# Third pair's rotation in an attention-and-experts kernel: VectorE sums GpSimd's products, and TensorE turns the pair one block later

## The chip, the cores and the metric

The kernel runs on one core of one Trainium2 chip. The core's engines have queues of their own and run beside each other: TensorE (PE in the rows, PEld for its weight loads), VectorE (DVE), ScalarE (ACT), GpSimd (POOL) and SyncE (SP, which here only issues transfers). Each queue is worked through in order, and an instruction whose input is late holds up all that stands behind it on its engine. The metric is the device time of one execution in microseconds (us), lower is better.

## The reference

Attention with rotary positions over 8 batches, 8 heads, 576 positions and 64 values per head, and a mixture-of-experts layer on its 4608 rows:

```python
def rotate(x):
    x1, x2 = (x[..., :half], x[..., half:])
    return np.concatenate([x1 * cos - x2 * sin, x1 * sin + x2 * cos], axis=-1)
q_rot, k_rot = (rotate(q), rotate(k))
scores = scale * np.matmul(q_rot, k_rot.transpose(0, 1, 3, 2))
scores = scores - np.max(scores, axis=-1, keepdims=True)
attn = np.exp(scores)
attn = attn / (np.sum(attn, axis=-1, keepdims=True) + 1e-09)
out = np.matmul(attn, v)
...
h_dense = np.maximum(x @ w1_dense, 0.0)
y_dense = h_dense @ w2_dense
expert_idx = np.argmax(logits, axis=1)
...
    h = np.maximum(x[mask] @ w1[e], 0.0)
    y_moe[mask] = gate_w[mask, None] * (h @ w2[e])
return y_dense + y_moe
```

## The kernel before, in words

The 64 heads are worked through as 32 pairs, `i` = 0 to 31. For each pair the steps are these.

- **Load**: `stage_load` brings q and k of two pairs at a time into a tile `qk` (SP's queue).
- **Rotation** (`stage_rope`): three products of `qk` with the tables `cosx` and `sinx` (lines 253, 254 and 255), in bf16, and their sum into the pair's tile `nat` (line 256). Pairs 0 and 1 are rotated by VectorE, with the products in a tile named `rab`; all others by GpSimd, with the products in tiles `ra` and `rb`, of which there is one each. There are three `nat` tiles, taken in turn.
- **Turn**: pairs 0, 1 and 2 are transposed by TensorE (`turn_first`, line 277, four pieces n = 0 to 3) and copied out by ScalarE (line 278) into `q1` and `k2`. From pair 3 on the turn is a transposing DMA (`stage_transpose`, line 263), and a second DMA moves the keys to their own tile (`stage_keys`, line 281, in the rows `k<-q`). Both are issued by SP.
- **First scores** (`s1_block`, lines 288 to 291): nine blocks `t` of query-major scores; VectorE takes the row maximum of each block (line 305, and 311 for the small piece of block 4). `s1_rest` does the last 64 keys (line 319), `join_max` the join (line 326). The blocks of the pairs up to 6 use four PSUM banks in turn: those tagged `s1` for even blocks, those tagged `ff` for odd ones and for the small piece of block 4.
- **Shift** (`shift_rows`): the maxima are turned by TensorE (line 333), fitted by ScalarE and VectorE (lines 337 and 338, tile `mT`) and written by an SP transfer (line 339) into two rows of `q1`, so that the second product subtracts them.
- **Second scores** (`s2_strip`, lines 346 to 349) with ScalarE's exponential (line 361), product with v (`av_part`, line 380) and scaling on VectorE (lines 391 and 392).

The order is written out by hand. `attention()` begins with two loops that do the first scores of pairs 0 and 1 and put the turns of pairs 1 and 2 between their blocks. After that the main loop runs over `i` and `t`: it does the first scores of pair `i + 2`, the second scores of pair `i` and the product with v of pair `i - 1`, and from the fifth turn or so fills TensorE with work of the dense and expert layers. The rotation of pair `i + 5` is put into GpSimd's queue at block 2 of turn `i`; those of pairs 3 and 4 stand ahead of the main loop. In this text **turn i** is one round of the main loop, and it is cut at the end of VectorE's join of maxima (line 326), which happens once per round.

Of the kernel before, what the change touches and what calls it, by code (L numbers as in the profile page):

```python
# [24 lines left out]
def kernel(  # L25
# [12 lines left out]
    nc = tc.nc  # L38
# [107 lines left out]
    state = {}  # L146
# [58 lines left out]
    def load(dst, src, b, hh):  # L205
        nc.sync.dma_start(dst.rearrange("p u (a j) d -> p (u a) (j d)", a=2)[:, :, 0:4 * D],
                          src[b, 4 * hh:4 * hh + 4, 0:MAIN, :].rearrange("h (p j) d -> p h (j d)", j=4))
        for a in range(2):
            nc.sync.dma_start(dst[64 * a:64 * a + 64, :, 4, :],
                              src[b, 4 * hh + a:4 * hh + a + 3:2, MAIN:S, :].rearrange("h p d -> p h d"))  # L210

    def stage_load(g, part):
        b, hh = divmod(g, 2)
        if part == 0:
            state["qk", g] = ap.tile([P, 2, 2, 10, D], f32, tag="qk", bufs=3, name="qk")
        load(state["qk", g][:, part], (q, k)[part], b, hh)
# [23 lines left out]
    def stage_rope(i):  # L240
        eng = nc.vector if i < 2 else nc.gpsimd
        g, u = divmod(i, 2)
        nat = nats[i % NAT].rearrange("p c w d -> p w c d")
        x = state["qk", g][:, :, u, 0:9]
        if i < 2:
            r = ap.tile([P, 5, DG], f32, tag="xn", bufs=2, name="rab").rearrange("p j d -> p (j d)")
            a, s = (r[:, n * 9 * D:(n + 1) * 9 * D].bitcast(bf16).rearrange("p (w c d) -> p w c d", w=2, d=D)
                    for n in range(2))
        else:
            a, s = (ap.tile([P, 2, 9, D], bf16, tag=n, bufs=1, name=n) for n in ("ra", "rb"))  # L250
        cx_ = cosx[:, None].broadcast_to([P, 2, 9, D])
        sx = sinx[:, None].broadcast_to([P, 2, 9, D])
        eng.tensor_tensor(a, x, cx_, AL.mult)  # L253
        eng.tensor_tensor(s[:, :, :, 0:half], x[:, :, :, half:D], sx[:, :, :, 0:half], AL.mult)  # L254
        eng.tensor_tensor(s[:, :, :, half:D], x[:, :, :, 0:half], sx[:, :, :, half:D], AL.mult)  # L255
        eng.tensor_tensor(nat, a, s, AL.add)  # L256

    A0, B0 = 0, S
# [8 lines left out]
    def turn_first(i, n):  # L267

        nat = nats[i % NAT]
        if n == 0:  # L270
            state["q1", i] = ap.tile([P, QC], bf16, tag="q1", bufs=NK, name="q1")
        c0, c1 = ((0, 4), (4, 9))[n // 2]
        w, dst = ((2, state["q1", i]), (1, k2s[i % NK]))[n % 2]
        r = w * D
        ps = pp.tile([P, 8, P], bf16, tag="ff" if w == 1 and i < 2 else "s2", bufs=2, name="nps")
        for c in range(c0, c1):
            nc.tensor.transpose(ps[0:r, c - c0], nat[:, c, 2 - w:2, :].rearrange("p w d -> p (w d)"), ident_b)
        nc.scalar.copy(dst[0:r, c0 * P:c1 * P], ps[0:r, 0:c1 - c0].rearrange("p c d -> p (c d)"))
# [15 lines left out]
    def s1_block(i, t):  # L294
        if t == 0:
            state["negm", i] = ap.tile([P, 10, 2], f32, tag="negm", bufs=3, name="negm")
        def bank(n):
            return "ff" if i < 7 and n % 2 else "s1"

        tag = bank(t)  # L300
        ps = pp.tile([P, MAIN], f32, tag=tag, bufs=2, name="s1")
        s1_mm(i, t, ps, 0)
        spend(512 if t != 4 else 800)
        banks[tag].append(took("dve", 0.6, product(0.22 if t != 4 else 0.32, tag)))
        nc.vector.tensor_reduce(state["negm", i][:, t, 0:1], ps, axis=AX.X, op=AL.max, negate=True)  # L305
        if t == 4:
            tag = bank(1)
            ps = pp.tile([P, MAIN], f32, tag=tag, bufs=2, name="s1")
            s1_mm(i, t, ps[:, 0:TAIL], 1)
            banks[tag].append(took("dve", 0.14, product(0.03, tag)))  # L310
            nc.vector.tensor_reduce(state["negm", i][:, t, 1:2], ps[:, 0:TAIL], axis=AX.X, op=AL.max, negate=True)
# [657 lines left out]
    MORE = 2900  # L969

    def attention():
        for i in range(2):
            for t in range(9):
                s1_block(i, t)
                if i == 0 and 2 <= t < 6:
                    turn_first(1, t - 2)
                if i == 1 and 3 <= t < 7:
                    turn_first(2, t - 3)
                if (i, t) == (1, 1):
                    shift_rows(0)  # L980
                    stage_load(3, 1)
                    dense = [load_w(n, w1d, moe_w1_dense) for n in range(DT)]
                    for u in range(HP):
                        cast_v(0, u)
            s1_rest(i)
            join_max(i)
        stage_rope(3)
        stage_rope(4)
        stage_transpose(3)
        AV = {2: (0, 2), 3: (2, 5), 6: (5, 7), 7: (7, 10)}  # L990
# [16 lines left out]
        for b in range(1, B):  # L1007
            for u in range(HP):
                i = 4 * (b - 1) + u - (b == 2)
                if b == 1:  # L1010
                    if u > 1:
                        when(u - 1, 6, 0, lambda u=u: stage_v(1, u, u + 1))
                    i, t = ((1, 8), (2, 4), (3, 3), (3, 8))[u]
                else:
                    when(i, 6, 0, lambda b=b, u=u: stage_v(b, u, u + 1))
                    i, t = i + 2, 3
# [6 lines left out]
        for b in range(B - 1):  # L1023
            s = 4 * b
# [60 lines left out]
        b, i = B - 1, NP - 1  # L1085
# [42 lines left out]
    with tc.manual_schedule():  # L1128
        load_pair(0, 0, nc.sync)
        load_pair(0, 1, nc.sync)  # L1130
        load_pair(1, 0, nc.sync)
        load_pair(1, 1, nc.sync)
        stage_load(1, 0)
        stage_load(1, 1)
        psi, sc = tables()
        nc.gpsimd.tensor_copy(ident_b, ident_f)
        nc.gpsimd.tensor_copy(ident_h, ident_f)
        for x in (cx, tops, gall):
            nc.gpsimd.memset(x, 0.0)
        gate_constants()  # L1140
        pad_tails()
        load_gate()
        pad_keys(0)
        tables_done(psi, sc)
        pad_keys(1)
        pad_keys(2)
        stage_v(0)
        stage_load(2, 0)
        stage_load(2, 1)
        stage_rope(0)  # L1150
        for n in range(4):
            turn_first(0, n)
        for x in range(3, NK):
            pad_keys(x)
        stage_rope(1)
        hold = const_p.tile([1, 1], bf16, name="hold")
        nc.gpsimd.tensor_copy(hold, nats[1][0:1, 0, 0, 0:1])
        stage_rope(2)
        stage_load(3, 0)
        setup_cm.__exit__(None, None, None)  # L1160
        attention()

        L = state["L"]
        n_rest = nc.values_load(L[-1][0:1, 0:1], min_val=0, max_val=B * (E - 1))
        with tc.If(n_rest > 0):
            for n in range(1, NREST + 1):
                with tc.If(n_rest >= n):
                    pick_rest(L, n)
                    picked()
                    load_rest()  # L1170
                    gate_rest(nc.vector, DT)
                    queue.extend(rest_items())
                    fill(1 << 30)
# [30 lines left out]
```

## Time and profile before

| what | us |
|---|---|
| median of three runs (lowest, highest) | 421.92 (421.78, 422.32) |
| the profiled execution, its own time | 423.38 |
| span of the profiled execution, first to last instruction | 421.80 |
| TensorE busy | 384.4 (91%) |
| VectorE busy | 332.5 (79%) |
| ScalarE busy | 307.4 (73%) |
| GpSimd busy | 295.7 (70%) |

The profile is of one execution. The shares are means over stages with different limits, so a change in one stage is read from that stage's rows. In a row of the timeline, the first number is the start after the span's first instruction, the second the length, and the bracket at the end is the idle time of the engine before it and what ended that.

### The profile page before, as it was taken

The page shows a single profiled execution, that of the slowest core. Times are in us where ns is not written, and L with a number is a line of the kernel's source. Part 1 is how long each engine was busy: PE and PEld are TensorE (multiplying, and loading weights), DVE is VectorE, ACT ScalarE, POOL GpSimd, SP SyncE. Part 2 cuts the span into 40 slices and gives each one's busy share as a digit, 9 for nine tenths or more (in the row PEclk, how much of TensorE's full clock was granted, in tenths as well). Part 3 has the DMA queues.
Part 4 walks back from the last instruction along what each step waited for, and adds up shares of the span by engine and source line. Part 5 has one row for each costly group of instructions (what it writes and reads, how often), then busy time and mean ns, then how long its engine had stood idle before and what let it go on. Part 6 is the DMA issues. An engine that isn't in the chain of part 4 may idle for free. (4 is left out here: it accounts for less than half of the span.)

```text
span 421.8 us, 11454 instructions
## 1 busy us (share of the span) xinstructions
PE 384.4 (91%) x4483; PEld 231.7 (55%) x4488; DVE 332.5 (79%) x794; ACT 307.4 (73%) x623; POOL 295.7 (70%) x212
## 2 busy tenths in 40 slices
PE   0777888998999999999999999999999899998992
PEld 0433455664665557565665556655656566566551
DVE  7987999999799888998799887988899777623740
ACT  7767787787868887788877886788777787774311
POOL 3499999999996999579984999299947000470220
PEclk9988999999999999999999999999999999999998
DMA  4995677699777996599587876698438910697842
GB/s 123 269 268 131 130 140 181 150 205 187 181 166 148 217 177 195 168 223 181 130 222 164 219 175 164 162 212 177 102 79 184 131 58 16 177 203 117 189 129 87
DMA packets 99329, 68.91 MB, mean 163 GB/s; under 512 B 55742, under 2 KB 91838, under 8 KB 99264
## 3 DMA queue, kind: packets, MB, share of 16 engines
q1 hardware_dynamic: 88928, 57.71, 54.8%
q0 software_dynamic: 10192, 10.23, 16.6%
q8 instruction: 37, 0.61, 0.6%
q14 instruction: 28, 0.23, 0.2%
q10 hardware_dynamic: 144, 0.13, 0.1%
HBM read 50.22 MB, written 14.42 MB: 153 GB/s over the span
## 5 line engine op out<-in xcount | busy, mean ns | idle before, releaser
L305 DVE TENSOR_REDUCE negm<-s 128x1 f32<-128x512 f32 x288 | 192.4, 684 | 38.1 <-PE s L291 36.5
L361 ACT ACTIVATE pm<-s 128x512 f16<-128x512 f32 x288 | 170.6, 600 | 58.5 <-PE s L349 50.9
L349 PE MATMUL s<-q,k 128*128 128x512 bf16 (+1 forms) x507 | 105.1, 286 | 5.7 <-ACT pm L361 3.8
L291 PE MATMUL s<-k,q 126*128 126x512 bf16 x256 | 98.2, 388 | 4.9 <-DVE negm L305 2.2
L253 POOL TENSOR_TENSOR ra<-qk,cosx 128x1152 bf16<-128x1152 f32 x30 | 78.8, 2627 | 2.9 <-DMA qk<-in_k_dram 1.4
L380 PEld LDWEIGHTS <-pm 128*128 128x128 f16 x1600 | 65.3, 98 | 24.9 <-issue 3.0
L256 POOL TENSOR_TENSOR nat<-ra,rb 128x1152 bf16<-128x1152 bf16 x30 | 70.9, 2363 | 2.4
L380 PE MATMUL av<-v,pm 128*128 128x65 f16 x1600 | 71.3, 194 | 0.5 <-DVE xn L392 0.3
L514 POOL DMA_DIRECT2D w1e<-in_moe_w_dram x8 | 6.4, 800 | 81.9 <-DVE early L811 38.0
L349 PEld LDWEIGHTS <-k 128*128 128x128 bf16 x512 | 36.9, 98 | 37.1 <-issue 10.4
L291 PEld LDWEIGHTS <-q 126*128 126x128 bf16 x512 | 35.4, 98 | 29.8 <-issue 9.7
L254 POOL TENSOR_TENSOR rb<-qk,sinx 128x576 bf16<-128x576 f32 x30 | 42.1, 1403 | 0.0
L255 POOL TENSOR_TENSOR rb<-qk,sinx 128x576 bf16<-128x576 f32 x30 | 42.0, 1400 | 0.0
L608 PE MATMUL yps<-w2e,he 128*128 128x512 f16 x124 | 36.7, 379 | 0.0
L608 PE MATMUL yps<-w2d,hd 128*128 128x512 f16 x124 | 36.5, 378 | 0.0
L557 PE MATMUL hps<-xh,w1d 128*128 128x512 f16 x128 | 35.9, 379 | 0.0
L557 PE MATMUL hps<-xg,w1e 128*128 128x512 f16 x128 | 35.6, 379 | 0.0
L591 POOL TENSOR_TENSOR xg<-xh,gB 128x2304 f16<-128x2304 f16 x7 | 32.1, 4584 | 1.9 <-ACT gB L531 1.6
L392 DVE TENSOR_TENSOR xn<-av,rz 128x320 f32<-128x320 f32 x64 | 31.5, 492 | 2.2
L370 ACT ACTIVATE pm<-s 128x64 f16<-128x64 f32 x64 | 26.2, 410 | 0.0
L612 ACT COPY y<-yps 128x512 f32<-128x512 f32 x31 | 18.2, 587 | 8.3 <-PE yps L608 7.8
L414 DVE TENSOR_TENSOR xl<-xps,xh 128x512 f16<-128x512 f32 x32 | 21.8, 682 | 3.0 <-ACT xh L410 3.0
(211 smaller groups left out, 559.3 us busy)
## 6 DMA issues: line engine op xcount, KB each, us to landing
out_dram<-y SPq DMA_DIRECT2D x31, 256.0 KB
qk<-in_q_dram SPq DMA_DIRECT2D x15, 512.0 KB
qk<-in_k_dram SPq DMA_DIRECT2D x15, 512.0 KB
vf<-in_v_dram SPq DMA_DIRECT2D x26, 256.0 KB
xTd<-xh SPq DMA_DIRECT2D x8, 576.0 KB
k<-q SPq DMA_DIRECT2D x29, 144.0 KB
w1e<-in_moe_w_dram POOLq DMA_DIRECT2D x8, 512.0 KB, 7.4
w2e<-in_moe_w_dram POOLq DMA_DIRECT2D x8, 512.0 KB, 8.9
```

The source lines that it names most:

```text
L253: eng.tensor_tensor(a, x, cx_, AL.mult)
L254: eng.tensor_tensor(s[:, :, :, 0:half], x[:, :, :, half:D], sx[:, :, :, 0:half], AL.mult)
L255: eng.tensor_tensor(s[:, :, :, half:D], x[:, :, :, 0:half], sx[:, :, :, half:D], AL.mult)
L256: eng.tensor_tensor(nat, a, s, AL.add)
L291: nc.tensor.matmul(out_ap, lhsT=qT[:, t * P:(t + 1) * P], rhs=kT[:, ka if t < 4 else kb], start=True, stop=True)
L305: nc.vector.tensor_reduce(state["negm", i][:, t, 0:1], ps, axis=AX.X, op=AL.max, negate=True)
L349: nc.tensor.matmul(out_ap, lhsT=kT[:, s * P:(s + 1) * P], rhs=qT[:, qa if s < 4 else qb], start=True, stop=True)
L361: nc.scalar.activation(state["pm", i][:, ORDER.index(s), 0:MAIN], ps, AF.Exp, scale=float(scale))
L380: nc.tensor.matmul(state["av"][:, x * VC:x * VC + D + 1], lhsT=state["pm", i][:, 4 * h + n if n < 4 else 8, q0:q0 + P], rhs=v16s[b % VB][: ...
L557: nc.tensor.matmul(st["ps"], lhsT=w[:, dt, ft * P:(ft + 1) * P], rhs=xh[:, dt, 0:MAIN], start=(dt == 0), stop=(dt == DT - 1))
L591: eng.tensor_tensor(xg[:, d], state["xh", key][:, d], state["gB", key][:, None, :].broadcast_to([P, DT // n, S]), AL.mult)
L608: nc.tensor.matmul(st["ps"], lhsT=h[:, ft, j * P:(j + 1) * P], rhs=w[:, ft, :], start=(n == 0), stop=(n == last))
```

## The change

The products of pair 2 stay on GpSimd but go into a `rab` tile of their own; their sum is made by VectorE, put behind the maximum of the first block of pair 1. The rotation of pair 3 now follows pair 2's products directly in the program. The first piece of pair 2's turn is moved from block 3 to block 4 of pair 1, so that two pieces stand behind block 4; the others stay where they were.

```diff
 def stage_rope(i):
         x = state["qk", g][:, :, u, 0:9]
-        if i < 2:
+        if i < 3:
             r = ap.tile([P, 5, DG], f32, tag="xn", bufs=2, name="rab").rearrange("p j d -> p (j d)")
...
         eng.tensor_tensor(s[:, :, :, half:D], x[:, :, :, 0:half], sx[:, :, :, half:D], AL.mult)
+        state["parts", i] = nat, a, s
+        if i != 2:
+            rope_add(i)
+
+    def rope_add(i):
+
+        eng = nc.vector if i < 3 else nc.gpsimd
+        nat, a, s = state.pop(("parts", i))
         eng.tensor_tensor(nat, a, s, AL.add)
...
     def attention():
+        ADD_AT = [(1, 0)]
         for i in range(2):
             for t in range(9):
                 s1_block(i, t)
                 if i == 0 and 2 <= t < 6:
                     turn_first(1, t - 2)
-                if i == 1 and 3 <= t < 7:
-                    turn_first(2, t - 3)
+                if (i, t) in ADD_AT:
+                    rope_add(2 + ADD_AT.index((i, t)))
+                for n in range(4):
+                    if (i, t) == (1, (4, 4, 5, 6)[n]):
+                        turn_first(2, n)
...
             s1_rest(i)
             join_max(i)
-        stage_rope(3)
         stage_rope(4)
...
         stage_rope(2)
+        stage_rope(3)
         stage_load(3, 0)
```

On VectorE, the stretch is the end of pair 0's maxima and the first blocks of pair 1. `s_318`, `s_321` and so on are the PSUM tiles of its blocks 0, 1, 2. Before:

```order
L319 TENSOR_REDUCE negm<-rest 128x2x4
L326 TENSOR_REDUCE m<-negm 128x18
L305 TENSOR_REDUCE negm<-s_318 128x1
L305 TENSOR_REDUCE negm<-s_321 128x1
L338 SCALAR_TENSOR_TENSOR mT<-up,low,mps 18x128
L305 TENSOR_REDUCE negm<-s_346 128x1
```

After the change the same stretch reads as follows (the line numbers are larger by 8, and the tiles have other numbers):

```order
L327 TENSOR_REDUCE negm<-rest 128x2x4
L334 TENSOR_REDUCE m<-negm 128x18
L313 TENSOR_REDUCE negm<-s_322 128x1
L264 TENSOR_TENSOR nat_80<-rab 128x2x9x64
L313 TENSOR_REDUCE negm<-s_326 128x1
L346 SCALAR_TENSOR_TENSOR mT<-up,low,mps 18x128
L313 TENSOR_REDUCE negm<-s_351 128x1
```

One instruction, the sum into `nat_80` (pair 2's tile), has come in between the maxima of blocks 0 and 1; nothing else moved on this engine.

On GpSimd, the stretch is the rotation of pairs 2 and 3 (`nat_80` and `nat_78`). Before:

```order
L1157 COPY hold<-nat_79 1x1
L253 TENSOR_TENSOR ra<-qk,cosx 128x1152
L254 TENSOR_TENSOR rb<-qk,sinx 128x18x32
L255 TENSOR_TENSOR rb<-qk,sinx 128x18x32
L256 TENSOR_TENSOR nat_80<-ra,rb 128x2x9x64
L253 TENSOR_TENSOR ra<-qk,cosx 128x1152
L254 TENSOR_TENSOR rb<-qk,sinx 128x18x32
L255 TENSOR_TENSOR rb<-qk,sinx 128x18x32
L256 TENSOR_TENSOR nat_78<-ra,rb 128x2x9x64
```

After:

```order
L1168 COPY hold<-nat_79 1x1
L253 TENSOR_TENSOR rab<-qk,cosx 128x1152
L254 TENSOR_TENSOR rab<-qk,sinx 128x18x32
L255 TENSOR_TENSOR rab<-qk,sinx 128x18x32
L253 TENSOR_TENSOR ra<-qk,cosx 128x1152
L254 TENSOR_TENSOR rb<-qk,sinx 128x18x32
L255 TENSOR_TENSOR rb<-qk,sinx 128x18x32
L264 TENSOR_TENSOR nat_78<-ra,rb 128x2x9x64
```

Pair 2's sum is gone from GpSimd, and all that stands behind it has moved up by one instruction. On TensorE eight rows (four weight loads and four transposes of `nat_80`, the first piece of the turn) have moved from ahead of the eight rows of pair 1's block 4 to behind them. ScalarE's and SP's orders are the same in both kernels.

## Rows read from the trace of the kernel before

**Rows 1.** Busy time of each engine in stretches: turns 0 to 4 of the main loop, then the long part that follows, then the end (us of the stretch, then for each engine busy us and the number of instructions; PEclk is the granted TensorE clock, 1.00 is full speed).

```profile
29.82:36.90 7.08, 4.75 (x36) 1.89 (x35) 6.64 (x13) 6.01 (x13) 7.00 (x4) 1.00 0.57 158
36.90:48.34 11.44, 9.75 (x97) 5.34 (x98) 8.30 (x18) 7.90 (x16) 11.13 (x7) 0.85 0.67 165
48.34:57.26 8.92, 7.73 (x97) 4.52 (x97) 8.51 (x19) 7.36 (x16) 8.76 (x5) 1.00 0.68 153
57.26:65.95 8.69, 7.73 (x97) 4.53 (x97) 8.52 (x20) 6.97 (x15) 8.53 (x7) 1.00 0.75 127
65.95:74.71 8.76, 7.73 (x97) 4.53 (x97) 8.51 (x19) 6.60 (x15) 8.60 (x6) 1.00 0.69 172
...
74.71:360.00 285.29, 279.72 (x3429) 172.49 (x3434) 242.28 (x577) 225.19 (x467) 213.90 (x122) 1.00 0.73 162
```

**Rows 2.** Timeline of TensorE: the end of turn 0 and the wait for pair 3's keys.

```profile
35.28 0.38 PE L349 MATMUL s<-q,k 128*128 128x512 bf16 x1
37.66 0.38 PE L291 MATMUL s<-k,q 126*128 126x512 bf16 x1 [2.00 <-DMA k<-q]
```

**Rows 3.** Timeline of GpSimd and of SP's queue (transfers issued): rotation of pairs 2 and 3, and pair 3's way to its keys.

```profile
16.09 2.62 POOL L253 TENSOR_TENSOR ra<-qk,cosx 128x1152 bf16<-128x1152 f32 x1 [1.37 <-DMA qk<-in_k_dram]
...
18.67 1.40 POOL L254 TENSOR_TENSOR rb<-qk,sinx 128x576 bf16<-128x576 f32 x1
...
20.02 1.39 POOL L255 TENSOR_TENSOR rb<-qk,sinx 128x576 bf16<-128x576 f32 x1
...
21.49 2.36 POOL L256 TENSOR_TENSOR nat<-ra,rb 128x1152 bf16<-128x1152 bf16 x1
...
23.93 2.62 POOL L253 TENSOR_TENSOR ra<-qk,cosx 128x1152 bf16<-128x1152 f32 x1
...
29.33 2.36 POOL L256 TENSOR_TENSOR nat<-ra,rb 128x1152 bf16<-128x1152 bf16 x1
...
31.72 1.41 SPq L263 DMA_TRANSPOSE q<-nat  x1
...
35.13 0.55 SPq L281 DMA_DIRECT2D k<-q  x1
```

**Rows 4.** Timeline of VectorE from the end of pair 0's maxima to the end of pair 1's.

```profile
21.46 1.28 DVE L305 TENSOR_REDUCE negm<-s 128x1 f32<-128x512 f32 x2
22.66 0.33 DVE L338 SCALAR_TENSOR_TENSOR mT<-up,low,mps 18x128 bf16<-18x128 bf16 x1
22.91 1.27 DVE L305 TENSOR_REDUCE negm<-s 128x1 f32<-128x512 f32 x2
24.68 0.69 DVE L305 TENSOR_REDUCE negm<-s 128x1 f32<-128x512 f32 x1 [0.50 <-PE s L289]
...
25.42 0.68 DVE L305 TENSOR_REDUCE negm<-s 128x1 f32<-128x512 f32 x1
26.49 0.69 DVE L305 TENSOR_REDUCE negm<-s 128x1 f32<-128x512 f32 x1 [0.39 <-PE s L291]
27.71 1.29 DVE L305 TENSOR_REDUCE negm<-s 128x1 f32<-128x512 f32 x2 [0.52 <-PE s L291]
28.91 0.68 DVE L319 TENSOR_REDUCE negm<-rest 128x8 f32<-128x512 f32 x1
29.63 0.19 DVE L326 TENSOR_REDUCE m<-negm 128x18 f32<-128x36 f32 x1
```

**Rows 5.** Timeline of VectorE: the sum of pair 0 and the instruction after it.

```profile
10.31 0.76 DVE L256 TENSOR_TENSOR nat<-rab 128x1152 bf16<-128x1152 bf16 x1
10.99 1.35 DVE L253 TENSOR_TENSOR rab<-qk,cosx 128x1152 bf16<-128x1152 f32 x1
```

**Rows 6.** Timeline of VectorE and GpSimd at the very start: an instruction of VectorE beside GpSimd's, and a later one of the same size with GpSimd idle.

```profile
2.24 0.28 POOL L1137 CAST ident_h<-ident_f 128x128 f16<-128x128 f32 x1
...
2.36 0.60 DVE L87 CAST theta<-pos_i 128x160 f32<-128x160 int32 x1
...
2.62 0.12 POOL L1139 MEMSET gall<- 128x40 f32 x1
...
5.46 0.24 DVE L104 TENSOR_SCALAR psi<-psi 128x160 f32<-128x160 f32 x1
```

**Rows 7.** Timeline of TensorE and ScalarE around the turn of pair 2: the waits, the copies and the first exponential.

```profile
23.90 0.40 PE L277 MATMUL nps<-ident_b,nat 128*128 128x128 bf16 x4 [1.59 <-POOL nat L256]
...
25.34 0.69 PE L277 MATMUL nps<-ident_b,nat 128*128 128x128 bf16 x5
...
22.20 2.61 ACT L238 CAST v<-vf 128x640 f16<-128x640 f32 x4
24.71 0.57 ACT L278 COPY q<-nps 128x512 bf16<-128x512 bf16 x1
...
29.15 1.66 ACT L361 ACTIVATE pm<-s 128x512 f16<-128x512 f32 x3 [1.30 <-PE s L349]
```

**Rows 8.** Transfers issued on SP's queue ahead of pair 3's transposing transfer.

```profile
23.66 0.81 SPq L339 DMA_DIRECT2D q<-mT  x1
...
26.30 2.01 SPq L176 DMA_DIRECT2D wf<-in_moe_w_dense_dram  x4
```

**Rows 9.** Busy time of each engine in two stretches, columns as in Rows 1: the granted clock after two quiet stretches of TensorE.

```profile
25.35:28.65 3.30, 3.30 (x22) 1.88 (x22) 2.39 (x6) 1.79 (x3) 3.30 (x3) 0.50 0.84 206
...
38.90:42.40 3.50, 3.47 (x34) 2.19 (x34) 2.32 (x6) 2.83 (x6) 3.42 (x3) 0.51 0.61 127
```

## The prediction, made blind

> **What bounds the kernel now.** I first read the busy times by stretch [rows 1]. In the long part from 74.71 to 360.00 us TensorE is busy 279.72 of 285.29 us: there it is the bound, and GpSimd (213.90 of 285.29) is not. So a change at the start can only move that whole part earlier or later. Turns 2 to 4 take 8.92, 8.69 and 8.76 us, with VectorE busy 8.51 or 8.52 in each: VectorE sets their pace. Turn 1 does the same work in 11.44 us, with VectorE busy only 8.30. It is the one slow turn, about 2.6 us over its neighbours.
>
> Next the timeline tells why. TensorE's last product of turn 0 starts at 35.28 and takes 0.38, so it is free at 35.66; pair 3's first product starts at 37.66, having waited 2.00 us for the keys' transfer [rows 2]. That transfer hangs on GpSimd [rows 3]: it works without a gap from 16.09, ends pair 3's sum at 29.33 + 2.36 = 31.69, and only then, at 31.72, SP issues the transposing transfer, at 35.13 the keys' transfer, which lands at 37.66. From the sum to the landing is 37.66 − 31.69 = 5.97 us. After the wait the granted clock is 0.51 from 38.90 to 42.40 [rows 9], which is 1.2 GHz. So turn 1 pays for late keys twice, and what makes them late is how long GpSimd's queue is.
>
> Third, VectorE in the stretch of the edit [rows 4]. From 21.46 to 29.82 it idles three times for TensorE: 0.50, 0.39 and 0.52, together 1.41 us. TensorE in turn waited 1.59 us for pair 2's sum (ready near 21.49 + 2.36 = 23.85) [rows 3, 7].
>
> **What the change removes.** Pair 2's sum leaves GpSimd: 23.93 − 21.49 = 2.44 us from its start to the next [rows 3]. Everything behind it moves up by that, unless something new holds GpSimd. Pair 3's sum would then end at 29.25. That alone puts the keys' landing at 35.22, ahead of the 35.66 at which TensorE is free.
>
> What that is worth: turn 1 falls from 11.44 to that of its neighbours, about 8.8 (between 8.69 and 8.92), which is −2.64 us. I take the stage and not the bare wait of 2.00, because the slow clock behind the wait goes as well. With the wait alone it would be −2.00.
>
> **What it adds.** One sum on VectorE, of a size that the trace shows: 0.76 us, the next instruction starting 0.68 after it [rows 5]. Behind it stand pair 1's remaining maxima and `mT`; who waits for them is TensorE (four PSUM banks) and SP (pair 0's shift).
>
> But this sum stands where no sum of VectorE has stood. Those of pairs 0 and 1 ran while GpSimd waited. This one is due when the first maximum leaves VectorE, 21.46 + 0.60 = 22.06 (two maxima take 1.28, one 0.68, so one starts every 0.60) [rows 4], and GpSimd has then begun pair 3's first product, at 21.49; such a product is followed by the next instruction 18.67 − 16.09 = 2.58 us later, so at 24.07 [rows 3]. The price is bounded from both sides:
> - Nothing is held up: the delay of VectorE is 0.68.
> - VectorE stands until that product ends: 24.07 − 22.06 + 0.68 = 2.69.
>
> The nearest row is one of the first microseconds [rows 6]: a VectorE cast of 160 elements beside GpSimd's work took 0.60, where an operation of its size with GpSimd idle took 0.24. The stretch of 0.36 is as long as the GpSimd work beside it: from its start at 2.36 to the end of the last of those, 2.62 + 0.12 = 2.74, is 0.38. So the row looks like an instruction that stood until its neighbour was done, and not like one that ran a bit slower. Taken as a rule it gives the upper bound, 2.69, and I take that. (GpSimd then loses about 0.7 to VectorE's sum in its turn.)
>
> The Trainium skill, page "SBUF — State Buffer", section "Who interferes with whom", says it outright: a VectorE instruction with both inputs in SBUF contends with a GpSimd instruction that reads SBUF, and the one that is issued second blocks until the first is done. No row here shows it for a sum beside a product. By that rule the result would be the forecast below; by the 0.36 of the row alone it would be that of the first rival.
>
> **The sum for the forecast.** VectorE's delay of 2.69 is first paid from the 1.41 us in which it idles [rows 4], if TensorE is ready earlier than now. It can be: the blocks no longer wait for a late turn, and the piece of block 4 needs only the bank of block 1. 2.69 − 1.41 = 1.28 us are left, by which turn 0 starts later. (TensorE could add some 0.3 to this: it stands still until near 25.4 and then may run at the low clock, as it does now from 25.35 [rows 9].) Turn 0 keeps its 7.08, since VectorE is busy 6.64 of it.
>
> Are the keys in time? TensorE is free at 35.66 + 1.28 = 36.94. Pair 3's sum ends at 31.69 − 2.44 + 0.7 = 29.95, so the keys land at 35.92. One queue comes in between: pair 0's shift was issued at 23.66 [rows 8], and its `mT` now ends near 22.66 + 0.33 + 2.69 = 25.68 [rows 4], so SP's transfers move back by 2.0. The last weight load ends at 28.31 + 2.0 = 30.3 instead of 28.31, 0.4 after the sum, and the keys land at 36.3 or, if the loads' data is in the way, up to 0.6 later. That is still no wait. So turn 1 takes 8.8.
>
> Net: +1.28 − 2.64 = −1.36 us. In the profiled execution that is 423.38 − 1.36 = 422.0 (span 420.4). That execution is 1.46 above the median of 421.92; I take the difference from the median, **420.6 us**. The rest of the run should only move: in it TensorE or VectorE is the bound, and GpSimd has room.
>
> **At no cost**: the turn of pair 2 one block later. ScalarE is busy with casts until 22.20 + 2.61 = 24.81 and copies the first piece at 24.71 [rows 7], so a piece that is ready earlier is not wanted. Without that cover, four transposes of 0.40 together would be the price. The tile of its own is free by then: pair 0's sum, its last reader, ended at 11.07 [rows 5]. Orders on ScalarE and SP are unchanged.
>
> **The rivals.**
> 1. *The sum is hardly held up* (delay 0.68, or 1.04 with the 0.36 of the row). It fits into the 1.41 us of idle time. For it: the row's stretch is small. Against: the row's GpSimd work was small too. Turn 0 then starts no later, perhaps 0.7 earlier, though not by more: the third piece of the turn starts at 25.34 and the copies before it cannot start before ScalarE's casts end [rows 7]. Time: 421.92 − 2.64 = 419.3, down to 418.6.
> 2. *The other side: GpSimd does not let go.* Its instructions follow each other without a gap, and if the next one is served ahead of the waiting sum, VectorE stands through it too. For it: the cast of [rows 6] seems to have stood through more than one of GpSimd's instructions. Through the second product it is 20.02 − 18.67 = 1.35 more: −1.36 + 1.35, 421.9. Through the third too, another 21.49 − 20.02 = 1.47: 423.4, slower. It decides from 25.4 us on: if the sum starts later than that, the gain is eaten.
> 3. *The gain is lost further on*, as when another transfer takes the wait's place in turns 2 to 5. For it: pair 4's keys follow the same path. Against: turns 2 to 4 show VectorE busy all the time. Time: about 421.5 to 422.
>
> **Chances.** What a measurement of this kernel can tell from no change is 0.2%, 0.84 us. The forecast has 0.50 (420.1 to 421.2, by 0.3 more from TensorE and −2.0 instead of −2.64 on one side, earlier keys on the other); the first rival 0.25; the second 0.15, a third of it within 0.84 of 421.92; the third 0.10. From these: faster 0.72 (0.45 of the forecast, 0.25 of the first rival, 0.02 of the third), same 0.17, slower 0.11. The range 418.8 to 421.8 leaves out most of the second rival, half of the third and the fastest end of the first, together about 2 in 10.
>
> **What would show it.** Right: VectorE's sum ends near 24.8, its record 2.7 us long or with idle time for GpSimd before it; GpSimd's second product for pair 3 starts about 0.7 late; no wait for `k<-q` in turn 1; turn 1 near 8.8 us at full clock; turn 0 starts about 1.3 later than 29.82. Wrong: a sum of 0.76 that starts at 22.1 (rival 1), or one that ends after 26 (rival 2); a wait for keys that is still there; a turn 1 of 11 us; or turns 0 to 4 shorter as said and the end not earlier (rival 3).

## The result, and the profile after

The change made the kernel slower. Over 22 runs of each, the median is 426.58 us (421.71 to 431.04) after and 422.84 us (419.67 to 427.54) before; the ratio is 1.0068, with a 95% interval of 1.004 to 1.0095. The ratios here leave disturbed runs out, the medians do not. The predicted time was 420.6, the range 418.8 to 421.8.

Two executions of the changed kernel were profiled: one of 429.06 us (span 427.5) and, as the first experiment, one of 426.25 us (span 424.7), which lies near the median. The second is shown unless the first is named. First the page (share of the span; in the last row busy us, mean ns, idle time before it) and the busy times of turns 0 to 2, columns as in [rows 1]:

```profile
span 424.7 us, 11458 instructions
PE 385.4 (91%) x4488; PEld 232.2 (55%) x4488; DVE 334.6 (79%) x795; ACT 308.0 (73%) x623; POOL 293.8 (69%) x211
...
L299 PE MATMUL s<-k,q 126*128 126x512 bf16 x256 | 98.3, 388 | 6.2 <-DMA k<-q 3.0
```

```profile
30.94:37.67 6.73, 4.49 (x35) 1.99 (x35) 6.64 (x13) 5.69 (x12) 6.57 (x5) 1.00 0.63 161
37.67:51.05 13.38, 10.75 (x97) 5.66 (x97) 8.47 (x18) 8.02 (x16) 13.14 (x8) 0.74 0.76 165
51.05:59.98 8.93, 7.74 (x97) 4.53 (x97) 8.51 (x20) 7.37 (x16) 8.77 (x5) 1.00 0.46 126
```

The engines do the same work. Turn 0 begins at 30.94 instead of 29.82 (+1.12) and is 0.35 shorter (6.73 for 7.08). Turn 1, which was to shrink to 8.8 us, has grown from 11.44 to 13.38 (+1.94). Turn 2 is as before (8.93 for 8.92). The sum, +1.12 − 0.35 + 1.94 = +2.71, is nearly all of the +2.9 of the span (424.7 for 421.8). In the first profile the pattern is the same and larger, with another 1.75 us (of 5.7) lost later, which was not traced:

```profile
31.58:38.31 6.73, 4.49 (x35) 2.00 (x35) 6.64 (x14) 5.69 (x12) 6.57 (x5) 1.00 0.82 163
38.31:52.29 13.98, 10.32 (x97) 5.49 (x98) 8.39 (x19) 8.01 (x16) 13.74 (x8) 0.76 0.68 155
```

The timeline of the second profile, in four pieces (GpSimd; VectorE; SP's queue; TensorE), is what answers to [rows 2 to 4, 8]:

```profile
21.03 2.61 POOL L253 TENSOR_TENSOR ra<-qk,cosx 128x1152 bf16<-128x1152 f32 x1
23.60 1.91 POOL L254 TENSOR_TENSOR rb<-qk,sinx 128x576 bf16<-128x576 f32 x1
...
26.94 2.36 POOL L264 TENSOR_TENSOR nat<-ra,rb 128x1152 bf16<-128x1152 bf16 x1
...
22.07 2.19 DVE L264 TENSOR_TENSOR nat<-rab 128x1152 bf16<-128x1152 bf16 x1
...
24.79 0.33 DVE L346 SCALAR_TENSOR_TENSOR mT<-up,low,mps 18x128 bf16<-18x128 bf16 x1
...
25.14 0.81 SPq L347 DMA_DIRECT2D q<-mT  x1
...
27.77 2.01 SPq L176 DMA_DIRECT2D wf<-in_moe_w_dense_dram  x4
29.89 2.10 SPq L271 DMA_TRANSPOSE q<-nat  x1
33.00 0.71 SPq L347 DMA_DIRECT2D q<-mT  x1
36.88 0.55 SPq L289 DMA_DIRECT2D k<-q  x1
...
39.40 0.59 PE L299 MATMUL s<-k,q 126*128 126x512 bf16 x1 [2.96 <-DMA k<-q]
```

VectorE's sum of 0.76 us has become a record of 2.19: it was due at 22.07, GpSimd had begun the long product at 21.03, and the sum ends at 24.26, 0.66 after GpSimd's next product starts. `mT` is 2.13 late (24.79 for 22.66), and with it pair 0's shift (25.14 for 23.66) and the loads behind it. Pair 3's sum ends at 26.94 + 2.36 = 29.30, 2.39 earlier than the 31.69 of before, and the transposing transfer is issued at 29.89 instead of 31.72. But the keys' transfer comes at 36.88 instead of 35.13: between the two lie 6.99 us where there were 3.41. From the keys' issue to TensorE's first product it is 2.52, as before (2.53). So TensorE waits 2.96, and then runs at the low clock:

```profile
39.40:42.90 3.50, 3.50 (x18) 1.70 (x19) 2.08 (x3) 2.20 (x4) 3.42 (x4) 0.50 0.96 241
```

From its first product to the end of the turn TensorE takes 51.05 − 39.40 = 11.65 us, and took 48.34 − 37.66 = 10.68. So of the +1.94, half (0.97) is the wait. The other half goes with the clock, which is at 1.2 GHz from the first product on (0.59 long, 0.38 before) and not only from 38.90 [rows 9], and comes back near 45.3, where it came back near 42.4 in the kernel before (mean clock of half-microsecond stretches: 0.73 in 45.00 to 45.50, 0.63 in 42.00 to 42.50).

The theory after this look: VectorE's stall is as forecast, and what went wrong is the transposing transfer, now issued while the loads are still moving. The rivals: VectorE's stall alone makes the keys late; the turn's new place does; or the kernel before would lose the same way once its sum came earlier.

### The profile page after: what moved, and what is told of

It is laid out like the page before. It is cut to its first block, busy times and chain, and to the rows that moved or that the text cites. A ratio compares the mean times of both kernels' runs of the same rounds, so it can differ in the third digit from the quotient of the medians.

```text
span 427.5 us, 11458 instructions
## 1 busy us (share of the span) xinstructions
PE 385.0 (90%) x4488; PEld 232.3 (54%) x4488; DVE 335.3 (78%) x795; ACT 307.6 (72%) x623; POOL 293.7 (69%) x211
## 5 line engine op out<-in xcount | busy, mean ns | idle before, releaser
L357 PE MATMUL s<-q,k 128*128 128x64 bf16 (+1 forms) x512 | 107.6, 288 | 5.6 <-ACT pm L369 3.7
L253 POOL TENSOR_TENSOR ra<-qk,cosx 128x1152 bf16<-128x1152 f32 x29 | 76.1, 2624 | 3.3 <-DMA qk<-in_k_dram 1.9
L264 POOL TENSOR_TENSOR nat<-ra,rb 128x1152 bf16<-128x1152 bf16 x29 | 68.6, 2364 | 2.3
L254 POOL TENSOR_TENSOR rb<-qk,sinx 128x576 bf16<-128x576 f32 x29 | 41.2, 1419 | 0.0
L255 POOL TENSOR_TENSOR rb<-qk,sinx 128x576 bf16<-128x576 f32 x29 | 40.6, 1400 | 0.0
L565 PE MATMUL hps<-xg,w1e 128*128 128x512 f16 x128 | 35.6, 379 | 0.0
```

Source lines behind the costliest of these rows:

```text
L357: nc.tensor.matmul(out_ap, lhsT=kT[:, s * P:(s + 1) * P], rhs=qT[:, qa if s < 4 else qb], start=True, stop=True)
L565: nc.tensor.matmul(st["ps"], lhsT=w[:, dt, ft * P:(ft + 1) * P], rhs=xh[:, dt, 0:MAIN], start=(dt == 0), stop=(dt == DT - 1))
```

## The experiments

"After" and "before" say which kernel the edit starts from. In the measured sentences "landing" is the start of TensorE's first product for pair 3, and "m0" to "m8" are the starts of VectorE's joins of maxima: m0 the one that begins turn 0, m1 the one that ends it, and so on. Before: m0 29.63, m1 36.71, m2 48.15, m3 57.07, m5 74.52, m7 96.54; after (second profile): 30.75, 37.48, 50.86, 59.79, 77.24, 99.25.

### e1: after, again

No edit.

> The changed kernel once more. In its first profile VectorE's sum stood 2.83 us, pair 0's shift was issued at 25.76, the weight loads at 28.39 to 30.40, pair 3's transposing transfer at 30.51, its keys' transfer only at 38.56, and TensorE waited 3.99 us. Theory T (transfers): the late part is the time that the transposing transfer takes while the delayed loads' data is still on the way, so it stays long here (6 to 8 us from issue to the keys' issue, against 3.4 before), and turn 1 is 12 us or more, ratio 1.004 to 1.010. Rival S (stall): the stall of VectorE is what costs; then the wait for keys may vary from run to run, and the time does not follow it.

Measured: 424.44 us median of 10 runs beside 422.72, ratio 1.0035 (0.9994 to 1.0076); these ten alone would not tell the loss from none. The profile is the one above.

### e6: the turn alone

```diff
 # before
-                if i == 1 and 3 <= t < 7:
-                    turn_first(2, t - 3)
+                for n in range(4):
+                    if (i, t) == (1, (4, 4, 5, 6)[n]):
+                        turn_first(2, n)
```

> The kernel before with only the turn of pair 2 moved one block later on TensorE. T and S alike: 0 to 0.3 us, since ScalarE copies the first piece only when its casts end (24.7); turn 0 starts within 0.4 us of the kernel before; ratio 0.998 to 1.002. If the moved turn were a cause of the loss, it shows here.

Measured: 421.82 us, ratio 0.9992 (0.9965 to 1.0019). m0 is 28.66, 0.97 earlier, and it is worth nothing:

```profile
31.68 1.41 SPq L263 DMA_TRANSPOSE q<-nat  x1
...
35.07 0.55 SPq L281 DMA_DIRECT2D k<-q  x1
...
37.59 0.38 PE L291 MATMUL s<-k,q 126*128 126x512 bf16 x1 [3.24 <-DMA k<-q]
```

The keys land when they landed before, and the wait is 1.24 longer instead. The turn's place is not the cause, and it was not quite without effect: it gives TensorE about 1 us, which the keys take back.

### e4: GpSimd waits for the sum

```diff
 # after
                 if (i, t) in ADD_AT:
                     rope_add(2 + ADD_AT.index((i, t)))
+                    hold2 = const_p.tile([1, 1], bf16, name="hold2")
+                    nc.gpsimd.tensor_copy(hold2, nats[2][0:1, 0, 0, 0:1])
+                    stage_rope(3)
...
-        stage_rope(3)
```

> The changed kernel, with GpSimd made to wait (a copy of one element of pair 2's tile) until VectorE's sum is done before it begins pair 3's products. The sum then has no neighbour: it should take 0.76 us and end at 22.8, mT near 23.7, and SP's transfers go out as in the kernel before (shift 23.7, loads until 28.3). GpSimd loses the 1.2 us of waiting: pair 3's sum ends near 30.4. T: the transposing transfer is issued at 30.4, about 1 us before the loads' data ends (31.5 before), takes 3.4 to 5 us, and the keys are late by 0 to 2 us; time 0.2 to 0.7% below the kernel before. S: with the stall gone the time is 2.6 us below the kernel before (ratio 0.994).

Measured: 422.19 us, ratio 0.9995 (0.9964 to 1.0026). Timeline (VectorE, GpSimd, SP, TensorE):

```profile
22.06 0.75 DVE L264 TENSOR_TENSOR nat<-rab 128x1152 bf16<-128x1152 bf16 x1
...
22.87 0.18 POOL L989 COPY hold<-nat 1x1 bf16<-1x1 bf16 x1 [1.72 <-DVE nat L264]
...
30.80 2.09 SPq L271 DMA_TRANSPOSE q<-nat  x1
...
34.37 0.55 SPq L289 DMA_DIRECT2D k<-q  x1
...
36.90 0.38 PE L299 MATMUL s<-k,q 126*128 126x512 bf16 x1 [1.19 <-DMA k<-q]
```

With GpSimd idle, the sum takes 0.75, and the whole loss is gone: m0 29.50, m2 46.45. The shift and the loads go out as before, the transfer is issued 0.92 earlier than before and takes 3.57, the landing is 36.90 (37.66 before), and turn 1 is 9.71 instead of 11.44. In its profile that is 1.7 us at m7 (94.83), but over ten runs the median gains only about 0.5 us, and the interval takes in 1. It is level with the kernel before.

### e8: the short products first

```diff
 # after
-        eng.tensor_tensor(a, x, cx_, AL.mult)
+        if i != 3:
+            eng.tensor_tensor(a, x, cx_, AL.mult)
...
+        if i == 3:
+            eng.tensor_tensor(a, x, cx_, AL.mult)
```

> The changed kernel, with pair 3's products in another order: the two short ones (1.40 us each) ahead of the long one (2.62). It tests how the sum's length is set. In three runs the sum ended 0.65 us after the next instruction of GpSimd could have begun behind the long product. If VectorE stands until the one product that is under way ends, the sum now takes 1.0 to 1.6 us instead of 2.2 to 2.8 (GpSimd's first short product begins at 21.0 to 21.6 and gives way 1.35 later). If the length of the delay were fixed, or set by the whole row of products, it would stay 2.2 or more. T for the time: the shift goes out 1.2 us earlier (near 24.0 to 24.5), the loads too, so the wait for keys shrinks by about that much or more, to 0 to 2 us; time 0 to 0.5% below the changed kernel's, near that of the kernel before or under it.

Measured: 424.31 us, ratio 1.0017 (0.9976 to 1.0058).

```profile
22.07 0.87 DVE L267 TENSOR_TENSOR nat<-rab 128x1152 bf16<-128x1152 bf16 x1
...
26.46 2.01 SPq L176 DMA_DIRECT2D wf<-in_moe_w_dense_dram  x4
29.26 1.74 SPq L274 DMA_TRANSPOSE q<-nat  x1
...
35.27 0.55 SPq L292 DMA_DIRECT2D k<-q  x1
...
37.89 0.38 PE L302 MATMUL s<-k,q 126*128 126x512 bf16 x1 [2.18 <-DMA k<-q]
```

A product of 1.39 us had begun at 20.94, and the sum took only 0.87. m0 is 29.54 and the weights are issued at 26.46 (26.30 before), so here the change has no side effect on VectorE or SP. Pair 3's sum ends at 26.87 + 2.36 = 29.23, as early as the prediction had it (29.25), and yet the landing is 37.89, no earlier than before (37.66): the transfer, issued 2.46 earlier, takes 6.01 instead of 3.41. **So an earlier sum alone gains nothing here**, in contrast to the prediction's 35.22, and the last rival above is half right. The loads are not all of the 2.60: their last packet ends at 32.26, and the keys are issued only 3.0 after it (more under e15). At m5 this profile is still level with the kernel before (74.72 and 74.52).

### e5: the transposing transfer behind pair 1's shift

```diff
 # after
-        stage_transpose(3)
...
+        when(0, 3, 0, lambda: stage_transpose(3))
```

> The changed kernel, with pair 3's transposing transfer put on SP's queue three blocks later (turn 0, block 3, behind pair 1's shift), when the weight loads' data should be done. T: issued near 34.3 instead of 30.5 or 29.9, it takes about 3.4 us to the keys' issue instead of 7 to 8, so the keys land near 40, no later than in the changed kernel (39.4 to 41.1) although the transfer was issued 4 us later. S or any theory in which the transfer's own time does not depend on what is on the way: it takes as long as in the changed kernel, and the keys land near 44.

Measured, one run: 428.77 us. The transfer was issued at 34.06, 4.17 later than in the changed kernel, and the keys at 37.39, only 0.51 later. Issued when the loads are through, it takes 3.33; nearly all of its 4 us of lead were spent waiting, for the loads or for what else follows under e16.

### e7 and e10: the weights later

```diff
 # e7 on after, e10 the same on before
-                    dense = [load_w(n, w1d, moe_w1_dense) for n in range(DT)]
...
-            when(i, t, 0, lambda part=part: cast_w(*part))
+        dense = []
+        for n in range(DT):
+            when(n, 7, 0, lambda n=n: dense.append(load_w(n, w1d, moe_w1_dense)))
+            when(n + 1, 5, 0, lambda n=n: cast_w(*dense[n]))
```

> The changed kernel, with the four weight loads taken away from in front of pair 3's transposing transfer: one each at block 7 of turns 0 to 3, cast at block 5 of the turns after. VectorE's sum, the shift and the turn are as in the changed kernel. T: the transposing transfer is issued near 30 and takes 3.4 us or a little more (the k loads of the qk group are still ahead), keys land near 36, no wait or one below 1 us, turn 1 8.8 us, turn 0 starts 1.0 to 1.7 late as in the changed kernel, time 0.2 to 0.4% below the kernel before. S: time stays above the kernel before.

> The kernel before, with the four weight loads moved in the same way as in the run with the weights later. T: the transposing transfer is issued at 31.7 as before and takes 3.4 us or less, since its data already went behind the loads; keys land at 37 to 37.7 and the wait of 1.5 to 2.0 stays; time within 0.3% of the kernel before. If the loads alone explain the gain of the other run, this one gains as much.

Measured, on after: 424.38 us, ratio 1.0053 (1.0025 to 1.008). SP's queue:

```profile
29.47 1.42 SPq L271 DMA_TRANSPOSE q<-nat  x1
33.46 0.70 SPq L347 DMA_DIRECT2D q<-mT  x1
34.27 0.55 SPq L289 DMA_DIRECT2D k<-q  x1
```

With 1 MB of weights out of the way, the keys are issued at 34.27, 2.61 earlier than in the changed kernel, as soon as SP has issued the shift. The wait is 0.5, and turn 1 takes 8.28 us (37.94 to 46.22). This is the gain that was predicted; but the weights, loaded in turns 0 to 3 instead, make turns 2 to 4 9.16, 9.06 and 9.52 long (8.92, 8.69 and 8.76 before), and m5 is 73.96, only 0.56 ahead of before. Turn 6 is longer too (12.30 for 11.01), but so it is in e14, where the weights stay. On before, the same edit gains hardly anything at the keys (34.84, landing 37.38) and costs as much: m5 75.70, ratio 1.005 (1.001 to 1.009). There the transfer is bound by GpSimd's sum; after the change it is bound by the loads.

### e2 and e3: the loads ahead of pair 0's shift

```diff
 # e2 on after, e3 the same on before
-                    shift_rows(0)
                     stage_load(3, 1)
                     dense = [load_w(n, w1d, moe_w1_dense) for n in range(DT)]
+                    shift_rows(0)
```

> The changed kernel, with the loads of pair 7's keys' group and of the four weight tiles put on SP's queue ahead of pair 0's shift instead of behind it, so that they no longer wait for mT. T: loads issued from 23.1, their data done before pair 3's sum (near 29.9); the transposing transfer, issued at 30.0, takes 3.4 us again, keys land near 36, no wait in turn 1, turn 1 8.8 us, time 1.3 below the kernel before (ratio 0.997). S: VectorE's stall is the same, so the time stays 0.4 to 1% above the kernel before.

> The kernel before, with the same two lines of SP's queue exchanged. T and S alike: pair 3's sum still ends at 31.7, so the keys' wait of 2.0 stays and the time is that of the kernel before within 0.3%. It is the control for the run with the loads first: what that one gains over the changed kernel must not be there in this pair.

Measured, on after: 426.0 us over runs from 419.8 to 429.1, ratio 0.9994 (0.9941 to 1.0048), which settles nothing. In the profile the wait for keys is gone and turn 1 takes 8.77, but the shift, 4.5 KB behind 1.5 MB, is late:

```profile
31.97 0.39 PE L357 MATMUL s<-q,k 128*128 128x512 bf16 x1 [1.66 <-DMA q<-mT]
```

Turn 0 is 8.70 instead of 6.73; m2 is 48.72. On before: ratio 1.0039 (1.0003 to 1.0075), the shift waited for 2.15, m2 48.32. The wait only moves from one transfer to another.

### e12, e13 and e11: the load of pairs 6 and 7 behind pair 3's keys

```diff
 # e12 on after, e13 on e8, e11 on before
-                    stage_load(3, 1)
...
-        stage_load(3, 0)
...
+        when(0, 4, 0, lambda: stage_load(3, 0))
+        when(0, 7, 0, lambda: stage_load(3, 1))
```

> The changed kernel with the same move of the loads of pairs 6 and 7. T: sum on VectorE 2.1 to 2.8 us, shift and weight loads still late by 2 us (weights issued from 25.9 to 28.0, data done near 30), transposing transfer issued near 29.5 and not held much: keys' issue at 33 to 34 instead of 36.9 to 38.6, no wait for keys or one under 1 us; turn 0 ends 0.8 to 1.6 us later than before and turn 1 ends 1.3 to 2 us earlier; ratio 0.994 to 0.998 if nothing further on gives it back. S: above 1.000.

> Both: pair 3's short products first (sum on VectorE 0.9 us instead of 2.2 to 2.8) and the loads of pairs 6 and 7 later. T: neither VectorE nor the transfer is held: transposing transfer issued near 29.3, keys' issue near 32.7, keys landed near 35.3, no wait; turn 1 ends 2.3 to 3 us earlier than before (near 45.5); ratio 0.992 to 0.996. It would be better than both kernels.

> The kernel before, with the loads of q and k for pairs 6 and 7 (0.5 MB each) moved from in front of pair 3's transposing transfer to behind pair 3's keys (turn 0, blocks 4 and 7). T: the weight loads' data is done near 29 to 30, so the transposing transfer finds an idle path; but it is still issued at 31.7, when pair 3's sum ends on GpSimd, so the keys' issue moves by under 0.5 us from 35.1, and the wait for keys stays at 1.5 to 2.0 us: ratio 0.998 to 1.002. If the transfers ahead were all that holds the keys in the kernel before, the wait would vanish here too.

Measured: ratios 1.0093 (1.0057 to 1.0129), 1.0085 (1.0049 to 1.012) and 1.0084 (1.0052 to 1.0117). The first two do what was wanted in turn 1, with keys issued at 34.39 and 34.37 and m2 at 46.83 and 46.39. Then the moved load collides with the next pair's transposing transfer, as in the second of them:

```profile
40.92 2.02 SPq L274 DMA_TRANSPOSE q<-nat  x1
...
46.29 0.55 SPq L292 DMA_DIRECT2D k<-q  x1
...
48.81 0.59 PE L302 MATMUL s<-k,q 126*128 126x512 bf16 x1 [3.73 <-DMA k<-q]
```

5.37 us from issue to keys; m3 is 60.67 (57.07 before). It is the same loss one pair later, and here nothing of it comes from VectorE. On before, too, pair 4's keys come 4.93 after the transfer (41.42 to 46.35).

### e14 and e17: half of that load behind the keys

```diff
 # e14 on e8, e17 on e4
-                    stage_load(3, 1)
...
+        when(0, 4, 0, lambda: stage_load(3, 1))
```

> Pair 3's short products first, and only the k loads of pairs 6 and 7 (0.5 MB) behind pair 3's keys; weights where they were. T: weights issued from 24.8 to 26.6, their data done near 29.5 to 30, transposing transfer issued near 29.3 and taking 3.4 to 5 us (keys' issue 32.7 to 34.4, against 35.3 with all loads ahead of it), wait for keys 0 to 1 us; turn 1 ends 1.5 to 2.5 us earlier than before. Pair 4's transfer has only this half to pass, so turn 2 should keep most of it: ratio 0.994 to 0.999.

> GpSimd waits for VectorE's sum as in the earlier run, and the k loads of pairs 6 and 7 go behind pair 3's keys. T: sum 0.76 us; pair 3's sum ends at 30.8, the transposing transfer finds the weights' data done and takes 3.4 us, keys' issue 34.2, keys landed 36.7, wait about 1 us as in that run (34.4 and 1.2): GpSimd's wait is what bounds here. Ratio 0.995 to 1.000.

Measured: 423.55 us, ratio 0.9995 (0.9951 to 1.0039), and 423.01 us, ratio 1.0013 (0.997 to 1.0056). Both profiles gain in turn 1 (m2 46.62 and 46.39), and over ten runs neither can be told from the kernel before. In the first, the transfer still takes 4.68 (29.87 to 34.55); in the second, issued at 30.80, it takes 3.40.

### e16: nothing else in the transfer's way

```diff
 # on e8, with the weights later as in e7
-                    stage_load(3, 1)
-                    dense = [load_w(n, w1d, moe_w1_dense) for n in range(DT)]
...
+        when(0, 4, 0, lambda: stage_load(3, 1))
```

> Pair 3's short products first, the weight loads at block 7 of turns 0 to 3, and half of the loads of pairs 6 and 7 behind pair 3's keys: nothing is left on the way when the transposing transfer is issued near 29.3. T: it takes 3.4 us as in the kernel before, keys' issue near 32.7, keys landed near 35.2, no wait; turn 1 ends near 45.5. If it takes 5 us or more all the same, what holds it is not the transfers ahead but something else, such as pair 1's shift behind it, or the time of its issue. The total will not show the gain, since the weights later cost 1 to 2 us in turns 2 to 6 in both earlier runs that had them.

Measured: 424.93 us, ratio 1.0036 (0.9992 to 1.008). SP's queue, and the stretches in which data moved (last column GB/s):

```profile
29.60 1.40 SPq L274 DMA_TRANSPOSE q<-nat  x1
32.37 0.67 SPq L350 DMA_DIRECT2D q<-mT  x1
34.53 0.54 SPq L292 DMA_DIRECT2D k<-q  x1
```

```profile
29.50:30.50 1.00, 0.90 (x4) 0.12 (x2) 0.97 (x3) 1.00 (x3) 0.92 (x2) 1.00 0.00 0
30.50:32.50 2.00, 1.56 (x11) 0.77 (x11) 2.00 (x5) 1.30 (x3) 2.00 (x2) 1.00 0.82 155
32.50:33.50 1.00, 0.62 (x7) 0.30 (x5) 1.00 (x3) 0.71 (x2) 1.00 (x1) 1.00 0.02 2
33.50:34.50 1.00, 0.75 (x9) 0.35 (x8) 1.00 (x4) 0.82 (x2) 1.00 (x2) 1.00 0.02 5
```

Nothing moves before the transfer, its data go through in 30.50 to 32.50, and then the keys are not issued for another 2 us. There is a second delay besides the loads. What was issued in between is pair 1's shift, at 32.37. The trace holds something else there: one packet of 16 KB on a queue that fetches instructions (q8), from 32.38 to 33.26. In the list of queues for 32.35 to 34.50 (packets, MB, share of 16 engines) it reads:

```profile
q8 instruction: 1, 0.02, 2.6%
```

The transposing transfer is closed by 32 packets of 4 bytes each; 30 of them come by 32.45, the last two only at 33.50, after the fetch.

### e15: pair 1's shift behind the keys

```diff
 # on e14
-        nc.sync.dma_start(state["q1", i][KR:P, :].rearrange("r (c p) -> r c p", p=P), mT)
+        def put():
+            nc.sync.dma_start(state["q1", i][KR:P, :].rearrange("r (c p) -> r c p", p=P), mT)
+        if i == 1:
+            state["put"] = put
+        else:
+            put()
...
         when(0, 4, 0, lambda: stage_keys(3))
+        when(0, 4, 0, lambda: state.pop("put")())
```

> The run before, and pair 1's shift is issued behind pair 3's keys instead of in front. It tells apart two readings of the runs in which the transposing transfer's data ended 2 us before it was reported done: if the shift, issued while that data is moving, is what holds the report, then here it comes 0.5 us after the data (keys' issue near 32.7); if it is the loads ahead, nothing changes against the run before (keys' issue within 0.5 us of that one).

Measured: 424.3 us, ratio 1.0039 (1.0008 to 1.0071).

```profile
29.47 1.42 SPq L274 DMA_TRANSPOSE q<-nat  x1
33.23 0.55 SPq L292 DMA_DIRECT2D k<-q  x1
33.88 0.69 SPq L351 DMA_DIRECT2D q<-mT  x1
...
47.44 0.58 PE L302 MATMUL s<-k,q 126*128 126x512 bf16 x1 [2.66 <-DMA k<-q]
```

3.76 us from issue to keys, 0.92 less than in e14 and 1.17 less than with a clear path. That the shift held the keys is not shown by it. In the kernel before and in e6, e10, e11 and e17 a shift stands between too, and the transfer takes 3.33 to 3.41. And in this profile the instruction fetch had also moved: it lies at 28.02 to 29.84, ahead of the transfer's data, where in e14 it lies at 31.97 to 32.91, in the midst of them.

For pairs 3 and 4, the packets in all these traces go with the fetch. Where the loads are through within 1 us of the transfer's issue and SP is not held by its own next instruction, pair 3's keys come 3.33 to 3.41 after it without a fetch beside the transfer's data (before, e5, e6, e10, e11, e17), and 4.39 to 5.03 with one (e3, e13, e14, e16). Where loads still move 1.5 us after the issue, the keys come 1.5 to 1.9 after the last load packet without a fetch (pair 3 in e4 and e15; pair 4 in e7, e11, e14, e15, e16 and e17), and 3.0 to 3.1 with one (e8 and both profiles of the changed kernel). A fetch that began only as the closing packets came held nothing (pair 4 in e12 and e13). No run moved the fetch on purpose, so this is a match and not a proof. The gain (m2 46.10) is lost again to pair 4's keys, as above.

## Why the prediction was wrong

**What bounds the kernel: half right.** Turn 1 pays for late keys, and a later or earlier start moves all the rest: so it was (turn 2 8.93; the span follows m3). But "what makes them late is how long GpSimd's queue is" was only one of two bounds that end at nearly the same time. The sum ended at 31.69, and the loads that SP had issued ahead were through just about then (367 GB/s in 29.50 to 31.50 of the kernel before, 84 in 31.50 to 33.50, last column):

```profile
29.50:31.50 2.00, 1.78 (x10) 0.44 (x8) 1.97 (x5) 1.67 (x5) 2.00 (x1) 1.00 0.99 367
31.50:33.50 2.00, 1.40 (x12) 0.59 (x9) 2.00 (x6) 1.50 (x5) 1.92 (x2) 1.00 0.34 84
```

e8 took the first bound away alone, and the landing stayed at 37.9, held by the loads and by the second delay.

**The price of the sum: right.** 2.69 of delay was taken, at the upper bound; `mT` came 2.13 and 2.75 late, with records of 2.19 and 2.83 (the latter with GpSimd's product begun at 21.64). The sum took 0.75 with GpSimd idle, and 0.87 to 1.51 where GpSimd was in a product of 1.4 us. The sum waits for the one product that is under way, and no more, so rival 2 fell, and so did rival 1. This agrees with the rule of the Trainium skill, page "SBUF — State Buffer", section "Who interferes with whom". GpSimd's next product took 1.91 instead of 1.40, the 0.5 that was put at 0.7. Turn 0 began 1.12 to 1.76 later, for a forecast of 1.28.

**The turn one block later: at no cost, as said**; alone it even gives 1 us, which is then waited away.

**"Are the keys in time?": this step failed.** It added 5.97 us, the time from sum to landing in the kernel before, to the new end of the sum, and allowed 0.4 to 1.0 more for the queue: 36.3 to 36.9. Measured: 10.10 us from the sum (29.30) to the landing (39.40), and 11.16 in the first profile (29.92 to 41.08). It treated the transfer's 3.4 us as a fixed length. It was 6.99 and 8.05 here: it depends on what is still moving when the transfer is issued, and on a second delay behind its data. The prediction had seen that the loads move back by 2.0 and that the sum comes 2.4 earlier, but compared the last load's *issue* (30.3) with the sum, not the time at which its data are through. In the second profile the data moved at these rates after the transposing transfer was issued at 29.89:

```profile
29.90:31.90 2.00, 1.62 (x8) 0.46 (x7) 1.97 (x5) 1.78 (x5) 2.00 (x1) 1.00 0.88 265
31.90:33.90 2.00, 1.38 (x10) 0.57 (x8) 2.00 (x5) 1.50 (x4) 2.00 (x3) 1.00 1.16 300
33.90:34.90 1.00, 0.76 (x4) 0.23 (x3) 1.00 (x4) 0.91 (x3) 0.92 (x2) 1.00 0.91 199
34.90:35.90 1.00, 0.99 (x14) 0.59 (x14) 0.94 (x3) 1.00 (x3) 1.00 (x1) 1.00 0.00 0
35.90:36.88 0.98, 0.54 (x10) 0.23 (x8) 0.98 (x3) 0.98 (x4) 0.98 (x1) 1.00 0.03 8
```

Four microseconds of loads come first; their last packet ends at 33.79. The burst in 33.90 to 34.90 has the rate at which the transposing data move in the kernel before (about 200 GB/s in 33.00 to 34.50), and behind it there are 2 us of silence until the keys are issued at 36.88. In the kernel before, the keys follow the end of the data by some 0.5 us. So the term of −2.64 was one of +1.94 (+2.54 in the first profile), and the sum +1.28 − 2.64 became +1.12 − 0.35 + 1.94.

Of the 3.58 by which the transfer grew (6.99 for 3.41), about 2.3 are the loads and about 1.3 the second delay. This is an estimate: without a fetch beside the data the keys came 1.5 to 1.9 after the last load packet (taken as 1.8), here 3.09 after it. With the loads alone the keys would then have been issued near 35.6, TensorE would have waited about 1.7, and with the clock as before the change would have cost some 0.5 us instead of 2.7. e8 lost 2.60 in this transfer with hardly a stall on VectorE; the stall, which put shift and loads back by 1.5 to 2.1, adds 1.0 to 2.0 more. So the loads took the gain; that it became a clear loss needs the second delay, whose cause is open. A fetch lies in its place in this profile too (34.53 to 35.64, with the last two closing packets at 35.62 and 35.63).

**The rivals.** The third named the right kind, "as when another transfer takes the wait's place", with a price that could not go past zero, since it asked only whether the gain would be lost. That the wait could grow beyond what it was, with the low clock from its end on, was in no case.

## What to carry to other kernels

The time from issue to landing of a transfer belongs to the moment at which it was issued: before moving an issue earlier, find when the data ahead of it on its queue are through, not when the last of it was issued. When one of two bounds that end together is removed, the gain is what lies between them, which may be nothing. And where an edit delays one small transfer at the head of a queue, all that stands behind it is delayed into whatever comes next.

## What was not expected of the hardware

- A transposing transfer issued when the loads were through took 3.33 us to the next step (e5), and 6.01 to 8.05 behind loads still in flight. With a clear path it could still take 4.93 (e16): its last two closing packets came 1.05 us after the others. A 16 KB instruction fetch beside the data fits all profiles looked at; that it is the cause was not tested.
- After the wait of 2.96 us the granted clock was 0.50 from the first product; after one of 2.00 the first product still ran at 0.38 us and the low stretch began at 38.90. The length of the wait alone does not settle it: after 3.24 us (e6) the first product also took 0.38, after 2.23 (e11) 0.58.
- Executions of one kernel differ by some 8 us (419.67 to 427.54 before). A gain of 1.7 us at m7 in a profile (e4) was not to be seen in ten runs.
